# The stacked left rows in one transfer each, and a table of attention pieces with a row per FFN pair

## The chip, the cores and the metric

The program runs on one core of one Trainium2 chip. The metric is the device time of one execution in microseconds (us); lower is better. Before the change it is 1098.47 us, the median of three runs (1098.16 to 1099.85).

Engines are named as in the profile: PE is the matrix engine (PEld its weight loads), DVE the vector engine, ACT the scalar engine, POOL the GpSimd engine, SP the engine that does nothing here but issue transfers. SP, ACT and POOL each issue DMA transfers into a queue of their own; the page calls SP's queue q1, ACT's q10 and POOL's q0.

## What is computed

One transformer block in float32 with its two branches in parallel, over 2048 tokens of 576 features:

```python
xn = _layernorm(x, axis=-1)
return x + _A_ref(xn, A_wqkv, A_wo) + _B_ref(xn, B_w1, B_b1, B_w2, B_b2)

# _A_ref: 32 heads of 18 features, each query sees 8 keys, two tokens apart
idx = pos[:, None] - off[None, :]            # off = arange(8) * 2
logits = jnp.where(mask[None, None, :, :], einsum("bhsd,bhswd->bhsw", q, kg) * scale, -1e9)
o = jnp.einsum("bhsw,bhswd->bhsd", softmax(logits), vg)      # then @ wo

# _B_ref: feed-forward (FFN) of 4608 hidden features, squared relu
h = jnp.einsum("bsd,df->bsf", x, w1) + b1
r = jnp.where(h > 0, h, 0)
out = jnp.einsum("bsf,fd->bsd", r * r, w2) + b2
```

## The kernel before

**Tiling.** The tokens are cut into four blocks of 512. Every float32 operand of a matmul is held as a high and a low part, and a product is made of three matmuls (high x high, high x low, low x high). The 576 features are 512 main ones, in four groups of 128, and 64 left over, the *left rows*.

**The FFN in pairs.** The 36 tiles of 128 hidden features are worked in 18 pairs (`ffn_pair`, L673), in two passes: pass 0 handles token blocks 0 and 1, pass 1 blocks 2 and 3. A pair makes its first-layer products by a scheme with seven block products in place of eight; the seven are called B11, T1, T2, T3, B21, B22 and T4, and come in this order (B22 and T4 change places in the first pair). Each is six matmuls of 128x512 (L698). Between them PE does the second layer of the pair before (L590), handed out by `work`. A pair takes about 17 us in pass 0.

**The left rows, stacked.** For pairs 0 to 2 (`PLAIN = 3`) the 64 left rows are added by matmuls of their own (L704). From pair 3 on, each of the seven products ends with one matmul more (L697, run at L698) whose 128 rows hold all four combinations of high and low parts of 32 left rows: `LW` is the weights' side, `ST` the tokens' side. The tokens' side is made once in a pass: `left_x` (L619) writes 64 rows of seven slots (one slot for each product, 512 numbers wide) to a DRAM scratch `stscr`, shown as `stk` in the profile, through POOL's queue. `load_stack` (L633) brings slots back to SBUF with every row twice: rows 0 to 63 into partitions 0 to 63, and the same rows into partitions 64 to 127. It is called in five places, from `part` (L706):

- pass 0, pair 1: slots 0 to 4 into a `kv` buffer (10,240 bytes a row), slot 5 into `xf` (2,048 bytes a row);
- pass 0, pair 2: slot 6 into `x4d` (2,048 bytes a row);
- pass 1, pair 1: slots 0 to 3 into a `w1r` buffer (8,192 bytes a row);
- pass 1, pair 2: slots 4 to 6 into the other `w1r` buffer (6,144 bytes a row).

`STACK` gives the slot of each product: T1 0, B11 1, B22 2, B21 3, T3 4, T2 5, T4 6. The first products that need the slots are those of pair 3 in each pass. The weights' side comes with `load_left_weights` (L655), tiles `mb`, `st` or `x`, read from a scratch shown as `lw`. Its source pattern also reads each row twice, but as `[NS * P, 2 * L], [0, 2], [1, n * P]`: 64 rows outermost, the repeat inside.

**What else the queues carry.** SP's queue carries, in program order, the second layer's weights (`w2r<-in_w`, L551, three buffers), in pass 0 also the first layer's weights (`w1r<-in_w`) and the stores of their split form (`w<-w1s`, L533) and of hidden tiles (`h<-r`, L777; `op<-h`, L766 and L769 in pass 1). ACT's queue brings the split first-layer weights back in pass 1 (`w1s<-w`, L536). POOL's queue carries attention's loads and stores and, in pass 0, the stores of the left weights (`lw<-st`, L652).

**The order on the engines** is written by hand: each engine runs its instructions in the order in which the kernel's code names them.

**Attention's pieces.** Attention runs on DVE (with one exponential on ACT for each group) as a generator, `attention` (L394), that is cut into 18 to 20 steps; `side(k)` (L441) runs the next k of them at the place in the order where it stands. Three tables set k: `PIECES[p]` at the start of pair p of pass 0, `SPOTS[p][i]` at six spots of pair p in pass 1 (`spot`, L793), and `LAST[k]` after step k of the block products behind pass 1 (`phase_blocks`, L1504). The spots of a pair lie after B11 and T1 (0), after T2 (1), after T3 (2), after B21 (3), after B22 (4) and at the end (5); in the first pair only spot 5 is used.

Of the kernel before, what the change touches and what calls it, by code (L numbers as in the profile page):

```python
# [8 lines left out]
F32 = mybir.dt.float32  # L9
# [10 lines left out]
TB = 512  # L20
# [12 lines left out]
L = P // G  # L33
# [9 lines left out]
NS = 7  # L43
PLAIN = 3
ROWS = {(4 * b - 1 + k // 3, k % 3): (b, h) for b in (2, 3) for k, h in ((0, 0), (2, 2), (3, 1), (5, 2), (6, 2))}
PIECES = (0, 0, 0, 2, 3, 4, 0, 3, 2, 0, 2, 2, 1, 0, 2, 2, 4, 5)
SPOTS = ('000001',) + ('110022', '110023', '110023', '110023') * 4 + ('110021',)
QUADS = ('01111110111110', '10100010101011', '00110111111111', '10010000111111', '00000000000001', '00110010101010')
LAST = '0000000000000111001010111111'
SINGLES = '12121212121200000000'  # L50
PAIRED = tuple(range(1, 16, 2))
SINGLE = tuple(p for p in range(NP) if p not in PAIRED)
# [7 lines left out]
def block_kernel(ctx: ExitStack, tc: tile.TileContext, x, xt, wqkv, wo, w1, b1, w2, b2, w1l, w2q, w2l, out):  # L60
    nc = tc.nc
# [53 lines left out]
    stscr = [dram.tile([2 * L, NS, TB], F32, name=f"stk{s}") for s in range(2)]  # L115
# [325 lines left out]
    def side(k, exp=True):  # L441

        while k > 0:
            if current[0] is None:
                if not queue or queue[0][0] not in landed:
                    return k
                name, make = queue.pop(0)
                current[:] = [make(), None, name]
                steps_done[0] = 0
            if current[1] == "exp" and not exp:  # L450
                return k
            try:
                current[1] = next(current[0])
                steps_done[0] += 1
                k -= 1
            except StopIteration:
                current[0] = None
        return 0
# [3 lines left out]
    def some_side(t):  # L462
        owed[0] += t
        while True:
            exp = current[1] == "exp"
            cost = COST[steps_done[0]] if current[0] is not None else COST[0]
            if owed[0] < cost / 2 or side(1):
                break
            owed[0] -= cost
            if exp or current[1] == "exp":  # L470
                break
# [128 lines left out]
    def dims(t, off, *ap):  # L600
        a = t[tuple(slice(0, 1) for _ in t.shape)]
        return bass.AP(tensor=a.tensor, offset=a.offset + off, ap=[*ap])
# [29 lines left out]

    def load_stack(s, t, i):  # L633
        n = min(t.shape[1], NS - i)
        for h in range(2):
            nc.sync.dma_start(t[2 * h * L:2 * (h + 1) * L, :n].bitcast(F32), stscr[s][:, i:i + n])
        for k, place in STACK.items():
            if i <= place < i + n:
                ST[k] = t[:, place - i]
# [33 lines left out]
    def ffn_pair(s, p, work, first=False):  # L673
# [32 lines left out]
        def part(i):  # L706
# [15 lines left out]
            if i == 2 - p and p in (1, 2) and s:  # L722
                load_stack(1, sb.tile([P, 4, TB], F32R, name="w1r", bufs=2), 4 * p - 4)
            if i == 2 and p == PLAIN - 1 and not s:
                load_stack(0, mt.tile([P, 1, TB], F32R, name="x4d"), 6)
# [7 lines left out]
            if (p, i) == (1, 2):  # L733
                load_stack(0, sb.tile([P, 5, TB], F32R, name="kv", bufs=3), 0)
                load_stack(0, sb.tile([P, 1, TB], F32R, name="xf"), 5)
# [57 lines left out]
        def spot(i):  # L793
            if s and (not first or i == 5):
                some_side(int(SPOTS[p][i]))

        if not first and not s:
            side(PIECES[p], False)
        spot(0)
# [276 lines left out]
    def load_h(s, p):  # L1076
        t = hs[s, p] = mt.tile([P, 2, 2, TB], F32R, name="h", bufs=3)
        nc.sync.dma_start(t[:, 1].rearrange("p f t -> p (f t)").bitcast(F32), hscr[s][p])
# [6 lines left out]
    def h_lo(s, p):  # L1085
        if p < NP:
            t = hs[s, p]
            tt(t[:, 1], t[:, 1].bitcast(F32), t[:, 0].bitcast(F32), ALU.subtract)
# [415 lines left out]
    def phase_blocks():  # L1504
# [28 lines left out]
        for k in range(len(ORDER)):  # L1533
# [54 lines left out]
            if k == 25:  # L1588
                load_h(1, SINGLE[1])
                h_hi(1, SINGLE[0])  # L1590
                h_lo(1, SINGLE[0])
            side(int(LAST[k]))
        load_h(1, SINGLE[2])
# [498 lines left out]
```

## Time and profile before

| what | value |
|---|---|
| median of three runs | 1098.47 us |
| the profiled execution's own time | 1099.84 us |
| its span, first to last instruction | 1098.1 us |
| PE busy | 1083.5 us, 4871 matmuls |
| DVE busy | 930.9 us (85%) |
| ACT, POOL busy | 570.7 us (52%), 160.0 us (15%) |
| granted TensorE clock, mean | 0.998 |
| DMA engines, mean busy share | 0.81 at 285 GB/s |

The profiled execution took 1.74 us more than its span and 1.37 us more than the median. The chain of work that ended last is PE's for 90% of the span. A row of a view names the line of the code, the engine, the operation and the tiles, `out<-in`; a tile has no buffer number, so `w1r` may be raw weights or, later, the stacked rows. "DMA share" is the mean over the core's 16 DMA engines. In the view of waits a row reads: engine, tile and line that waited `<-` what ended the wait: us in total, times, longest.

### The profile page before, as it was taken

The page shows a single profiled execution, that of the slowest core. Times are in us where ns is not written, and L with a number is a line of the kernel's source. Part 1 is how long each engine was busy: PE and PEld are TensorE (multiplying, and loading weights), DVE is VectorE, ACT ScalarE, POOL GpSimd, SP SyncE. Part 2 cuts the span into 40 slices and gives each one's busy share as a digit, 9 for nine tenths or more (in the row PEclk, how much of TensorE's full clock was granted, in tenths as well). Part 3 has the DMA queues.
Part 4 walks back from the last instruction along what each step waited for, and adds up shares of the span by engine and source line. Part 5 has one row for each costly group of instructions (what it writes and reads, how often), then busy time and mean ns, then how long its engine had stood idle before and what let it go on. Part 6 is the DMA issues. An engine that isn't in the chain of part 4 may idle for free.

```text
span 1098.1 us, 13935 instructions
## 1 busy us (share of the span) xinstructions
PE 1083.5 (99%) x4871; PEld 908.9 (83%) x4871; DVE 930.9 (85%) x1245; ACT 570.7 (52%) x800; POOL 160.0 (15%) x294
## 2 busy tenths in 40 slices
PE   9999999999999999999999998999999999999998
PEld 7998888888888888888799986888778888887887
DVE  7976899999988979999899676879688888888986
ACT  5545655666656564555344344555455555543332
POOL 5011220212130100003110301021021040000110
PEclk9999999999999999999999999999999999999999
DMA  8758997897998697876865989998988988566573
GB/s 284 256 198 304 302 403 275 320 356 285 328 342 311 222 387 238 282 247 219 304 219 164 359 299 308 383 334 333 377 291 327 361 322 313 177 206 213 203 235 100
DMA packets 106887, 312.53 MB, mean 285 GB/s; under 512 B 12865, under 2 KB 39489, under 8 KB 95169
## 3 DMA queue, kind: packets, MB, share of 16 engines
q1 hardware_dynamic: 70048, 198.75, 51.5%
q0 software_dynamic: 15584, 71.96, 18.0%
q10 hardware_dynamic: 21184, 40.94, 11.1%
q8 instruction: 38, 0.62, 0.2%
q14 instruction: 33, 0.26, 0.1%
HBM read 216.62 MB, written 94.98 MB: 284 GB/s over the span
## 4 chain that ended last, share of the span: by engine, by line
PE 90%; DVE 5%; DMA 3%; issue 1%; ACT 1%; POOL 0%; ACTq 0%; DVEq 0%; POOLq 0%
PE p L590 35%; PE p L698 34%; PE p L1187 9%; PE p L1514 6%; PE p L1843 2%; DMA w1s<-w 2%; PE p L1191 2%; DVE pr L128 1%; PE p L1898 1%; PE p L704 1%; DMA w2r<-in_wo 1%; DVE h L128 1%; PE p L1753 1%; DVE w2s L128 0%; DVE r L128 0%
## 5 line engine op out<-in xcount | busy, mean ns | idle before, releaser
L590 PE MATMUL p<-h,w2s 128*128 128x512 f32 x1618 | 389.6, 390 | 0.0
L590 PEld LDWEIGHTS p<-h,w2s 128*128 128x128 f32 x1618 | 303.7, 188 | 64.3 <-ACT h L749 0.5
L698 PE MATMUL p<-X,w1s 128*128 128x512 f32 x864 | 219.6, 390 | 1.5 <-DVE r L128 1.5
L698 PEld LDWEIGHTS p<-X,w1s 128*128 128x128 f32 x864 | 162.2, 188 | 35.8 <-DVE r L128 1.9
L698 PE MATMUL p<-S,w1s 128*128 128x512 f32 x648 | 167.2, 394 | 0.5 <-ACT p L786 0.5
L698 PEld LDWEIGHTS p<-S,w1s 128*128 128x128 f32 x648 | 121.1, 189 | 29.3 <-ACT r L806 2.9
L562 ACT ACTIVATE w2s<-w2r 128x640 fp32r<-128x640 f32 x132 | 96.7, 734 | 87.2 <-PE p L590 54.1
L434 POOL DMA_DIRECT2D o<-q x128 | 69.4, 620 | 466.3 <-DVE q L128 465.8
L128 DVE TENSOR_TENSOR w2s<-w2r,w2s 128x576 fp32r<-128x576 f32 (+1 forms) x133 | 99.8, 751 | 18.0 <-ACT w2s L562 17.8
L745 ACT ACTIVATE r<-r,b1t 128x512 f32<-128x512 f32 x72 | 52.1, 724 | 116.1 <-DVE r L128 114.1
L128 DVE TENSOR_TENSOR h<-h 128x1024 fp32r<-128x1024 f32 (+1 forms) x74 | 72.5, 989 | 21.3 <-ACT h L762 13.7
L128 DVE TENSOR_TENSOR pr<-lg,kv 128x1152 f32<-128x1152 f32 x64 | 86.7, 1355 | 1.3
L128 DVE TENSOR_TENSOR pr<-q,kv 128x1152 f32<-128x1152 f32 x64 | 86.7, 1355 | 1.1
L405 DVE TENSOR_REDUCE lg<-pr 128x64 f32<-128x1152 f32 x64 | 86.4, 1350 | 1.0
L128 DVE TENSOR_TENSOR r<-p,r 128x512 f32<-128x512 f32 (+2 forms) x81 | 55.0, 681 | 36.2 <-ACT r L831 18.2
L128 DVE TENSOR_TENSOR pr<-pr 128x576 f32<-128x576 f32 (+1 forms) x128 | 77.5, 605 | 3.1
L753 ACT ACTIVATE r<-r 128x1024 f32<-128x1024 f32 x56 | 59.2, 1057 | 0.9
L806 ACT ACTIVATE r<-p 128x512 f32<-128x512 f32 x36 | 21.5, 598 | 57.2 <-PE p L698 57.1
L128 DVE TENSOR_TENSOR w1s<-w1r,w1s 128x1024 fp32r<-128x1024 f32 (+2 forms) x42 | 46.2, 1102 | 5.6 <-ACT w1s L523 5.0
L831 ACT ACTIVATE r<-p 128x512 f32<-128x512 f32 x36 | 21.5, 599 | 54.1 <-PE p L698 54.1
L745 ACT ACTIVATE r<-p,b1t 128x512 f32<-128x512 f32 x72 | 48.2, 671 | 0.0
L128 DVE TENSOR_TENSOR h<-r,h 128x1024 fp32r<-128x1024 f32 (+2 forms) x35 | 39.9, 1146 | 7.6 <-ACT r L753 6.0
(263 smaller groups left out, 1488.2 us busy)
## 6 DMA issues: line engine op xcount, KB each, us to landing
kv<-kvq POOLq DMA_DIRECT2D x32, 1296.0 KB, 9.6
w2r<-in_w SPq DMA_DIRECT2D x112, 320.0 KB, 4.1
w<-w1s SPq DMA_DIRECT2D x21, 1024.0 KB, 7.1
w1s<-w ACTq DMA_DIRECT2D x19, 1024.0 KB, 8.0
h<-r SPq DMA_DIRECT2D x28, 512.0 KB, 6.5
h<-h SPq DMA_DIRECT2D x28, 512.0 KB, 4.0
w<-w1s SPq DMA_DIRECT2D x15, 768.0 KB, 9.4
w1s<-w ACTq DMA_DIRECT2D x15, 768.0 KB, 7.7
```

What stands on the lines that cost most here:

```text
L128: return nc.vector.tensor_tensor(out=out, in0=a, in1=b, op=op)
L405: nc.vector.tensor_reduce(out=lg[:, j * HG:(j + 1) * HG].rearrange("p a w -> p w a"), in_=pr.rearrange("p w (a d) -> p w a d", d=DH), axis ...
L434: nc.gpsimd.dma_start(rows[:, i], q[i * L:(i + 1) * L, :, a:z])
L562: nc.scalar.activation(w2s[stream[i]][:, :DE], raw2[i], AF.Copy)
L590: nc.tensor.matmul(yp[b][c], v, a, start=c not in yb[b], stop=c in last and c not in [o[0] for o in ops[i + 1:]], skip_group_check=True)
L698: nc.tensor.matmul(to, l, r, start=start and i == 0, stop=i == len(mm) - 1, skip_group_check=True)
L745: nc.scalar.activation(to, a, AF.Relu, bias=b1t[:, f:f + 1])
L753: nc.scalar.activation(r, r, AF.Square)
L1187: nc.tensor.matmul(to, l[:, js], r, start=start and n == 0, stop=n == len(mm) - 1, skip_group_check=True)
L1191: nc.tensor.matmul(to, v[:, js], ws[LEFT, f][:, n], start=False, stop=n == 1, skip_group_check=True)
L1514: nc.tensor.matmul(p, l, r, start=id(p) not in begun, stop=stop, skip_group_check=True)
L1843: nc.tensor.matmul(p[:, :QW], l, r, start=k == 0, stop=k == len(mm) - 1)
```

## The change

There are two edits. The first makes one transfer of the two halves in `load_stack`: the source pattern reads the 64 rows, then the same 64 rows again (a step of 0, twice, outermost), into all 128 partitions of the tile. The same bytes move; the five calls issue five transfers in place of ten. The second edit changes the three tables that place attention's pieces: one number of `PIECES` (pair 14), one place of `LAST`, and `SPOTS`, which becomes a row for each of the 18 pairs. Pass 1 gets 115 steps where it had 114, the block products one fewer.

```diff
-PIECES = (0, 0, 0, 2, 3, 4, 0, 3, 2, 0, 2, 2, 1, 0, 2, 2, 4, 5)
-SPOTS = ('000001',) + ('110022', '110023', '110023', '110023') * 4 + ('110021',)
+PIECES = (0, 0, 0, 2, 3, 4, 0, 3, 2, 0, 2, 2, 1, 0, 3, 2, 4, 5)
+SPOTS = ('000002', '110022', '110023', '010023', '110023', '110022', ...
...
-        for h in range(2):
-            nc.sync.dma_start(t[2 * h * L:2 * (h + 1) * L, :n].bitcast(F32), stscr[s][:, i:i + n])
+        nc.sync.dma_start(t[:, :n].rearrange("p s c -> p (s c)").bitcast(F32),
+                          dims(stscr[s], i * TB, [0, 2], [NS * TB, 2 * L], [1, n * TB]))
```

`dims` builds an access pattern by hand, a list of (step, count) from the outermost to the innermost; `L` is 32.

The first place is SP's queue in pass 0, around pair 1 and 2. `kv`, `xf` and `x4d` are the stacked rows, `mb` and `x` the left weights of pairs 3 and 4, `w` and `h` stores to DRAM. Before:

```order
L643 DMA st<-in_w1l 128x512
L636 DMA kv<-stk_150 64x2560 x2
L636 DMA xf<-stk_150 64x512 x2
L663 DMA mb<-lw_152 128x1x896
L777 DMA h_162<-r_1274 128x1024
L551 DMA w2r<-in_w 128x640
L533 DMA w_116<-w1s 128x2048
L551 DMA w2r<-in_w 128x640
L506 DMA w1r<-in_w 128x1024
L533 DMA w_117<-w1s 128x1536
L636 DMA x4d<-stk_150 64x512 x2
```

And now:

```order
L643 DMA st<-in_w1l 128x512
L635 DMA kv<-stk_150 128x1x2560
L635 DMA xf<-stk_150 128x1x512
L663 DMA mb<-lw_152 128x1x896
L777 DMA h_162<-r_1274 128x1024
L551 DMA w2r<-in_w 128x640
L533 DMA w_116<-w1s 128x2048
L551 DMA w2r<-in_w 128x640
L506 DMA w1r<-in_w 128x1024
L533 DMA w_117<-w1s 128x1536
L635 DMA x4d<-stk_150 128x1x512
```

Nothing has changed places; each pair of 64-row transfers is one of 128 rows.

The second place is SP's queue in pass 1, pairs 1 and 2, where both `w1r` are the stacked rows and `st` is the left weights of pair 3. Before:

```order
L551 DMA w2r<-in_w 128x640
L636 DMA w1r<-stk_151 64x2048 x2
L663 DMA st<-lw_152 128x1x896
L636 DMA w1r<-stk_151 64x1536 x2
L766 DMA op_157<-h 128x2048
```

And now:

```order
L551 DMA w2r<-in_w 128x640
L635 DMA w1r<-stk_151 128x1x2048
L663 DMA st<-lw_152 128x1x896
L635 DMA w1r<-stk_151 128x1x1536
L766 DMA op_157<-h 128x2048
```

Here too the order is the same, with four transfers become two.

The third place is DVE in pass 1, from the sum behind B22 of pair 9 (the first `r<-p,r`) to the sum behind T3 of pair 10 (the second one), which frees the bank that B22 of pair 10 writes: `sm` and `lg` are attention's softmax, `pr` its products, `h<-h` the low parts of hidden tiles, `w2s` that of the second layer's weights. Before:

```order
L128 TENSOR_TENSOR r_6717<-p_6659,r_6698 128x512
L128 TENSOR_TENSOR h<-h 128x512 x2
L416 TENSOR_REDUCE sm<-lg 128x32
L417 RECIPROCAL sm<-sm 128x32
L128 TENSOR_TENSOR lg<-lg,sm 128x256
L128 TENSOR_TENSOR pr<-lg,kv 128x1152
L128 TENSOR_TENSOR q<-pr 128x144
L128 TENSOR_TENSOR h<-h 128x512 x2
L128 TENSOR_TENSOR pr<-lg,kv 128x1152
L128 TENSOR_TENSOR w2s<-w2r,w2s 128x576
L128 TENSOR_TENSOR r_6831<-p_6763,r_6807 128x512
```

And now:

```order
L128 TENSOR_TENSOR r_6714<-p_6654,r_6693 128x512
L416 TENSOR_REDUCE sm<-lg 128x32
L417 RECIPROCAL sm<-sm 128x32
L128 TENSOR_TENSOR lg<-lg,sm 128x256
L128 TENSOR_TENSOR pr<-lg,kv 128x1152
L128 TENSOR_TENSOR q<-pr 128x144
L128 TENSOR_TENSOR h<-h 128x512 x2
L128 TENSOR_TENSOR pr<-lg,kv 128x1152
L128 TENSOR_TENSOR h<-h 128x512 x2
L128 TENSOR_TENSOR w2s<-w2r,w2s 128x576
L128 TENSOR_TENSOR r_6829<-p_6766,r_6804 128x512
```

The first two `h<-h` stood ahead of the softmax and one product step; now they stand behind them. (The additions `pr<-pr` between a `pr<-lg,kv` and its `q<-pr` are left out in both.)

More of the change, by code (lines that the diff above doesn't have):

```diff
@@ L45 @@
 ROWS = {(4 * b - 1 + k // 3, k % 3): (b, h) for b in (2, 3) for k, h in ((0, 0), (2, 2), (3, 1), (5, 2), (6, 2))}
-PIECES = (0, 0, 0, 2, 3, 4, 0, 3, 2, 0, 2, 2, 1, 0, 2, 2, 4, 5)
-SPOTS = ('000001',) + ('110022', '110023', '110023', '110023') * 4 + ('110021',)
+PIECES = (0, 0, 0, 2, 3, 4, 0, 3, 2, 0, 2, 2, 1, 0, 3, 2, 4, 5)
+SPOTS = ('000002', '110022', '110023', '010023', '110023', '110022', '110023', '100024', '010024', '120022', '110023', '110023', '110023', '110022', '110023', '110023', '110123', '010021')
 QUADS = ('01111110111110', '10100010101011', '00110111111111', '10010000111111', '00000000000001', '00110010101010')
-LAST = '0000000000000111001010111111'
+LAST = '0000000000000111001010011111'
 SINGLES = '12121212121200000000'
```

## Prediction

> **What bounds the kernel now.** I read the page's first part, then the view of PE's waits (who waited `<-` for what: us in total, times, longest).
>
> ```profile
> span 1098.1 us, 13935 instructions
> PE 1083.5 (99%) x4871; PEld 908.9 (83%) x4871; DVE 930.9 (85%) x1245; ACT 570.7 (52%) x800; POOL 160.0 (15%) x294
> PE p L704 <- DMA w1s<-w: 4.0, 1, 4.0
> PE p L1187 <- DVE h L1063: 2.0, 1, 2.0
> PE p L698 <- DVE r L128: 1.5, 1, 1.5
> PE p L698 <- ACT p L786: 0.5, 1, 0.5
> ```
>
> PE works through 99% of the span, so the matmuls bound the kernel and no edit here takes one away. PE's waits are few and single: the longest, 4.0 us, is for a transfer, and 1.5 + 0.5 us of the others lie in pass 1. So a gain is a few us at most, while a loss has no such limit: any transfer that lands late stops PE one for one.
>
> The timeline of PE and that of the queues show the long wait in its place, pass 1, beside the stacked rows.
>
> ```profile
> 651.82 0.33 SPq L551 DMA_DIRECT2D w2r<-in_w  x1
> 652.37 1.40 SPq L636 DMA_DIRECT2D w1r<-stk  x2
> 655.71 0.33 ACTq L536 DMA_DIRECT2D w1s<-w  x1
> 656.54 0.55 SPq L663 DMA_DIRECT2D st<-lw  x1
> 657.19 1.20 SPq L636 DMA_DIRECT2D w1r<-stk  x2
> 662.49 0.33 ACTq L536 DMA_DIRECT2D w1s<-w  x1
> 669.71 0.72 PE L704 MATMUL p<-x,w1s 128*128 128x512 f32 x2 [4.03 <-DMA w1s<-w]
> 674.36 0.33 ACTq L536 DMA_DIRECT2D w1s<-w  x1
> 686.22 0.39 PE L698 MATMUL p<-w1r,st 128*128 128x512 f32 x1
> 667.00:680.00 13.00, 10.29 (x38) 8.33 (x39) 6.82 (x12) 1.90 (x3) 1.13 (x3) 0.87 1.01 319
> ```
>
> The weights issued at 655.71 land 14 us later, behind a full set of DMA engines, and PE waits 4.03 us for them. The last row (from the table by windows; the columns behind the busy times are granted clock, DMA share and GB/s) shows what such a wait costs beyond itself: the clock was 0.87 over 13.0 us, 13.0 x 0.13 = 1.7 us more.
>
> The cause lies in the halves. In pass 0 the same load stands nearly alone, and the DMA view of 130 to 150 us gives busy share and GB/s in 40 slices of 0.5 us:
>
> ```profile
> 127.28 0.33 SPq L643 DMA_DIRECT2D st<-in_w1l  x1
> 127.72 1.14 SPq L636 DMA_DIRECT2D kv<-stk  x2
> 128.91 1.31 SPq L636 DMA_DIRECT2D xf<-stk  x2
> 130.33 0.57 SPq L663 DMA_DIRECT2D mb<-lw  x1
> DMA  8996999996799999999999999979999999999999
> GB/s 246 246 266 143 246 246 225 184 246 127 152 256 309 255 331 414 426 398 418 478 442 414 406 449 449 430 316 487 415 413 418 385 430 442 430 410 365 352 254 306
> 136.87 0.55 POOL L652 DMA_DIRECT2D lw<-st  x1 [17.25 <-ACT st L607]
> 142.52 0.39 PE L698 MATMUL p<-kv,mb 128*128 128x512 f32 x1
> 156.85 0.39 PE L698 MATMUL p<-x4d,mb 128*128 128x512 f32 x1
> 130.00:136.00 6.00, 6.00 (x28) 4.95 (x28) 5.80 (x11) 4.53 (x7) 0.00 (x0) 1.00 0.97 215
> ```
>
> While the 64-row halves move, the 16 engines are 0.97 busy and yet move 215 GB/s; from the 15th slice on they are as busy and move about 416 GB/s, 26 GB/s for one engine. Half of the partitions take half the rate, so a transfer to all 128 could run twice as fast, if all 16 engines carry it.
>
> **What decides: how many engines carry the new transfer.** [...] The new source pattern is 2 x 64 x a row, with the count of 2 outermost; the tile's is 128 x a row. What the DMA view tells of how transfers are dealt out, and of the packets of SP's queue and of all:
>
> ```profile
> DMA packets 179, 0.61 MB, mean 197 GB/s; under 512 B 16, under 2 KB 16, under 8 KB 144
> mb<-lw SPq DMA_DIRECT2D x1, 448.0 KB, 8.2
> q1 hardware_dynamic: 70048, 198.75, 51.5%
> DMA packets 106887, 312.53 MB, mean 285 GB/s; under 512 B 12865, under 2 KB 39489, under 8 KB 95169
> ```
>
> The first row is the DMA view of 186.0 to 189.1 us, in which one `w2r` of 128 rows ends: 16 small packets stand beside its rows, one for each engine, I take it. All large transfers of before have 32, 64 or 128 as their outermost count on both sides, `mb<-lw` too, which repeats each row inside of 64. So no row prices a count of 2; the ends are 16 engines and 2. The nearest row by bytes is `mb<-lw`, but it differs in exactly the outermost count. I take 2, since the cut that the pattern itself offers first gives two shares of 64 rows, and dealing the inner 64 out would need another rule for this case than for the rest. This is a choice, and its chance below says so.
>
> [...]
>
> **The change part by part, with two engines.** Each engine then carries half of the bytes at 26 GB/s. All transfers of SP's queue wait behind their share on those two engines, as in before each landed behind its forerunner.
>
> Two rows of the DMA view, for the times from issue to landing (KB each, median us), are used below:
>
> ```profile
> w2r<-in_w SPq DMA_DIRECT2D x1, 320.0 KB, 9.1
> st<-in_w1l SPq DMA_DIRECT2D x1, 256.0 KB, 2.7
> ```
>
> *Pass 0.* The stack is issued at 127.72; `st<-in_w1l` alone landed after 2.7 us of which 262,144 bytes at 416 GB/s are 0.6, so about 2 us pass before data move: 129.7. Slots 0 to 4 are 128 x 10,240 bytes, 655,360 for each engine: 25.2 us. Slot 5: 131,072, 5.0 us. `mb<-lw`, 458,752 bytes over 16, 28,672: 1.1 us, and two `lw<-st` of the same size between them 2.2 us (the second is issued 3 us behind the first). Together 33.5: landing at 163.2. The first matmul that needs both starts at 142.52: PE waits **20.7 us**, and the clock costs **1.7** more. Next is `x4d`: behind it stand `h`, three weight loads, two stores and its own 5.0 us, 13.6 in all, 176.8; it is needed at 156.85 + 20.7 = 177.6, so nothing is added, with 0.8 us to spare. The other transfers behind (`w2r`, `w`) are needed a pair (17 us) later and move along with PE.
>
> *Pass 1.* The queue ahead is full until the `w2r` of 651.82 lands, 9.1 us later: 660.9. Then slots 0 to 3, 524,288 bytes an engine, 20.2 us; `st` 1.1; slots 4 to 6, 393,216, 15.1; and from ACT's queue, which shares the engines, two loads of 65,536 and one of 49,152, 5.0 + 1.9. Together 43.3: 704.2. T2 of pair 3 needs slot 5 at 686.22: **18.0 us**, again with **1.7** of clock. The old wait at 669.71 stays inside this sum: that load has its own queue and lands sooner, but what PE gains there it waits out at T2.
>
> *The five issues saved* are 0.5 to 0.7 us each on SP, which is not the late one: 0.
>
> *Moved pieces.* The 1.5 us wait is B22 of pair 10 waiting for DVE's sum behind T3. DVE's timeline there:
>
> ```profile
> 785.35 1.42 DVE L128 TENSOR_TENSOR h<-h 128x512 f32<-128x512 f32 x2 [4.80 <-ACT h L762]
> 794.01 0.68 DVE L128 TENSOR_TENSOR r<-p,r 128x512 f32<-128x512 f32 x1
> ```
>
> DVE stood idle 4.80 us for `h<-h`, with the softmax queued behind it. The new order puts softmax and product ahead of `h<-h`, into that idle time, and only one more group of additions (1.55 us) ahead of the sum. The wait should go: **-1.5**, bounds -2.0 (the 0.5 us wait goes too) and +4 (each product step is 1.36 us, and one or two of the other moved steps may land ahead of a sum that PE needs).
>
> Sum: 20.7 + 1.7 + 18.0 + 1.7 - 1.5 = 40.6 us. Made against the profiled execution, 1099.84 + 40.6 = 1140.4; that execution is 1.37 above the median, so **1139.1 us**.
>
> Bounds. The highest slices but two, 449 GB/s, give 28 for one engine: waits of 18.3 and 14.9, no loss of clock, -2.0: 1129.7. The mean rate of SP's queue, 198.75 MB in 51.5% of 16 x 1098.1 us, is 22.0: waits of 26.9 and 25.9, 3.4 of clock, 0 for the pieces: 1154.7. The likeliest case by itself: 1129 to 1155.
>
> **The rivals.**
>
> *Sixteen engines, faster.* Speaks for it: rate and share above. The place is the 4.03 us wait at 669.71. Slots 0 to 3 are 1.05 MB, 4.9 us at 215 and 2.5 at 416; the second load's part ahead of the weights saves some 0.7. The weights land 3.1 us sooner, the wait shrinks to about 1, and the clock loss goes (the 2.0 us wait in the first fence left the clock at 1.00): 3.1 + 1.7 + 1.5 = 6.3, **1092.2 us**, 1091 to 1097. Against it: the count of 2. It decides from about eight engines: slots 0 to 5 are then 7.6 us, `mb` lands at 140.6, before 142.52.
>
> *Sixteen engines, no change.* The bytes stay, DMA is 1.01 busy there with or without, and the wait may only move to the next load. **1098 us**, 1096.5 to 1100.5.
>
> *The pieces cost.* The transfers are harmless, but a product step of 1.36 us stands ahead of a sum in some of the 16 pairs: three such, **1102.5 us**.
>
> **How the numbers follow.** Two engines 0.67, sixteen and faster 0.21, no change 0.08, the pieces 0.04. A measurement of this kernel can tell 0.2%, 2.2 us, from no change. So faster 0.21, same 0.08, slower 0.71. The range must reach over both signs: 1091 to 1155 leaves out the ends of the first two cases, about 1 in 10 or a little more.
>
> **What would show each step.** With two engines the page's small packets ("under 512 B") fall by 10 x 16 - 5 x 2 = 150 to 12,715; with sixteen by 80, to 12,785. PE's waits should name `kv<-stk` or `mb<-lw` with some 20 us, and `w1r<-stk` with some 18, and the wait for `w1s<-w` and that for DVE's `r` be gone; the stacked loads should land 25 to 45 us after issue. It is wrong if they land within 8 us, or if they land late and PE does not wait.

## The result, and the profile after

The changed kernel takes 1157.63 us, the median of 4 runs (1155.99 to 1159.1), beside 1099.16 us (4 runs) for the kernel before: a ratio of 1.0524, with an interval of 1.0493 to 1.0555. The forecast was 1139.1 us, 1091 to 1155: right in its direction and in the two engines, but too low; the result lies above its range. The profiled execution took 1157.96 us, its span 1156.3.

The page of the changed kernel; the first number behind a queue's kind is its packets:

```profile
span 1156.3 us, 13924 instructions
PE 1087.2 (94%) x4871; PEld 912.7 (79%) x4871; DVE 931.9 (81%) x1245; ACT 571.0 (49%) x800; POOL 160.0 (14%) x294
DMA packets 106736, 312.53 MB, mean 270 GB/s; under 512 B 12714, under 2 KB 39338, under 8 KB 95018
q1 hardware_dynamic: 69898, 198.75, 48.8%
```

SP's queue went from 70,048 packets to 69,898, which is 150 fewer: ten transfers with a small packet for each of 16 engines became five with one for each of two. So two engines carry each of the new transfers. The records of landings in the trace say the same: that of `kv<-stk` comes in two parts, at 161.97 and 162.18 us, where those of other transfers come in sixteen. PE is busy 3.7 us longer than the 1083.5 of before, and 94% of the span in place of 99%; the rest is waits. PE's waits, all that the view lists:

```profile
PE p L698 <- DMA mb<-lw: 28.7, 1, 28.7
PE p L698 <- DMA st<-lw: 19.3, 1, 19.3
PE p L698 <- DMA w1r<-stk: 14.8, 1, 14.8
PE p L1670 <- DVE lg L1663: 2.1, 1, 2.1
```

Three waits for transfers stand where there was one of 4.0 us; that one, the 2.0 us for `h` and the 1.5 and 0.5 us are gone. These four make 64.9 us. With the 2.1 us wait, which was there before too, and two of 0.7 and 0.2, the old ones made 11.0. So 53.9 us of the 58.2 that the span grew are waits and 3.7 are PE's longer busy time.

Where they lie is shown by the timelines of the changed kernel, SP's issues (start, us that the issue took) and PE's first matmuls behind each wait:

```profile
128.57 0.64 SPq L635 DMA_DIRECT2D kv<-stk  x1
129.27 0.53 SPq L635 DMA_DIRECT2D xf<-stk  x1
129.90 24.06 SPq L663 DMA_DIRECT2D mb<-lw  x1
154.06 5.10 SPq L777 DMA_DIRECT2D h<-r  x1
...
682.70 0.56 SPq L635 DMA_DIRECT2D w1r<-stk  x1
683.45 2.37 SPq L663 DMA_DIRECT2D st<-lw  x1
685.92 1.91 SPq L635 DMA_DIRECT2D w1r<-stk  x1
694.38 26.27 SPq L766 DMA_DIRECT2D op<-h  x1
```

```profile
172.07 0.80 PE L698 MATMUL p<-kv,mb 128*128 128x512 f32 x1 [28.68 <-DMA mb<-lw]
725.05 0.76 PE L698 MATMUL p<-w1r,st 128*128 128x512 f32 x1 [19.32 <-DMA st<-lw]
745.24 0.79 PE L698 MATMUL p<-w1r,st 128*128 128x512 f32 x1 [14.83 <-DMA w1r<-stk]
```

Pair 3 of pass 0 starts its first stacked product at 172.07 in place of 142.52. The transfers that PE waits for first in each pass are ordinary ones, `mb<-lw` and `st<-lw`: they land in sixteen parts, but two of the sixteen come behind the stacked rows. Of `st<-lw`, fourteen parts were there by 691.77 us and the last two at 723.35 and 724.92; the two parts of the stacked load ahead of it landed at 722.23 and 723.50. The issues of 24.06 and 26.27 us were not foreseen: SP itself stood still while the stacked rows ahead of them in its queue were being worked off (0.58 us for `mb<-lw` in the kernel below that has the load in ACT's queue).

The table by windows (the last three columns are granted clock, DMA share, GB/s) and the DMA view of 128 to 175 us (KB each, median us from issue to landing):

```profile
130.00:136.00 6.00, 6.00 (x29) 4.95 (x28) 5.11 (x10) 4.46 (x7) 0.00 (x0) 1.00 0.16 61
150.00:154.00 4.00, 0.00 (x0) 0.00 (x0) 0.00 (x0) 0.00 (x0) 2.76 (x6) 0.50 0.35 99
160.00:172.00 12.00, 0.00 (x0) 0.00 (x0) 0.00 (x0) 0.00 (x0) 0.00 (x0) 0.50 0.98 323
```

```profile
kv<-kvq POOLq DMA_DIRECT2D x1, 1296.0 KB, 12.7
lw<-st POOLq DMA_DIRECT2D x2, 448.0 KB, 7.1
mb<-lw SPq DMA_DIRECT2D x1, 448.0 KB, 42.1
o<-q POOLq DMA_DIRECT2D x4, 48.0 KB, 5.2
o<-q POOLq DMA_DIRECT2D x4, 24.0 KB, 8.4
```

In the window of 130 to 136 us, where the halves had the engines busy at 0.97 for 215 GB/s, it is now 0.16 and 61 GB/s, about two engines' worth. `mb<-lw` lands 42.1 us after its issue; fourteen of its sixteen parts were there by 162.65 us, the last two at 171.69 and 172.02. And POOL's attention transfers, `kv<-kvq` and eight `o<-q`, run in the same stretch: their packets take turns with the stacked rows on the two engines (those of `kv<-kvq` end there at 164.97 us, on the fourteen others before 160.1), and the forecast's sum did not hold them.

### The profile page after: what moved, and what is told of

It reads as the page before. It is cut to its first block, busy times and chain, and to the rows that moved or that the text cites. A ratio compares the mean times of both kernels' runs of the same rounds, so it can differ in the third digit from the quotient of the medians.

```text
span 1156.3 us, 13924 instructions
## 1 busy us (share of the span) xinstructions
PE 1087.2 (94%) x4871; PEld 912.7 (79%) x4871; DVE 931.9 (81%) x1245; ACT 571.0 (49%) x800; POOL 160.0 (14%) x294
## 2 busy tenths in 40 slices
DMA packets 106736, 312.53 MB, mean 270 GB/s; under 512 B 12714, under 2 KB 39338, under 8 KB 95018
## 3 DMA queue, kind: packets, MB, share of 16 engines
q1 hardware_dynamic: 69898, 198.75, 48.8%
## 4 chain that ended last, share of the span: by engine, by line
PE 88%; DMA 9%; another core or an unknown queue 1%; DVE 1%; issue 0%; POOL 0%; ACT 0%; POOLq 0%; SPq 0%; ACTq 0%
PE p L590 34%; PE p L698 30%; PE p L1187 9%; PE p L1514 8%; DMA mb<-lw 4%; DMA st<-lw 4%; PE p L1843 2%; DMA w1s<-w 2%; PE p L1191 2%; PE p L1753 1%; PE p L1898 1%; PE p L704 0%; PE p L1670 0%; DVE lg L405 0%; DVE pr L128 0%
## 5 line engine op out<-in xcount | busy, mean ns | idle before, releaser
L698 PE MATMUL p<-X,w1s 128*128 128x512 f32 x864 | 219.7, 390 | 0.2
L698 PEld LDWEIGHTS p<-X,w1s 128*128 128x128 f32 x864 | 162.1, 188 | 34.7 <-ACT r L745 0.5
L698 PE MATMUL p<-S,w1s 128*128 128x512 f32 x648 | 169.0, 397 | 0.0
L698 PEld LDWEIGHTS p<-S,w1s 128*128 128x128 f32 x648 | 122.7, 192 | 28.8 <-ACT r L806 2.7
L128 DVE TENSOR_TENSOR h<-h 128x1024 fp32r<-128x1024 f32 (+1 forms) x74 | 72.6, 990 | 19.0 <-ACT h L762 10.7
L806 ACT ACTIVATE r<-p 128x512 f32<-128x512 f32 x36 | 21.5, 598 | 75.3 <-PE p L698 75.1
L786 ACT ACTIVATE p<-p 128x512 f32<-128x512 f32 x36 | 20.9, 582 | 64.8 <-PE p L698 62.3
L374 POOL DMA_DIRECT2D kv<-kvq x32 | 18.6, 587 | 205.5 <-DVE pr L128 161.4
```

The costliest lines, as they stand in the source:

```text
L128: return nc.vector.tensor_tensor(out=out, in0=a, in1=b, op=op)
L698: nc.tensor.matmul(to, l, r, start=start and i == 0, stop=i == len(mm) - 1, skip_group_check=True)
```

## The experiments

The theory is that the outermost count of the source sets how many engines carry a transfer, that all that is queued on these few comes late, and that PE waits for that. Lines from L630 on are moved by up to four in some of these kernels (L702 is then L698). The kernel before was run beside each: medians of 1098.5 to 1099.2 us, 1100.2 in the last.

### Each edit alone

The first edit with the old tables (`e_load`), and the second with the two halves (`e_pieces`); the diffs are the two parts of the diff above.

> The one-transfer load alone, with the old tables. Theory: all of the loss stays, 1156 to 1161 us, with PE waiting some 29 us before pair 3 of pass 0 and some 34 us in pass 1; page q1 has 69,898 packets. Rival (part of the loss is the pieces'): 1120 to 1150 us.

> The new tables of attention's pieces alone, with the stacked rows in two 64-row transfers as before. Theory (two DMA engines carry the new transfers, and that is the whole loss): the tables cost nothing and remove the wait of 1.5 us for DVE's sum in pair 10, so 1095 to 1098 us. Rival (the moved pieces bring part of the loss): 1101 us or more.

The new load alone: 1162.15 us (ratio 1.0573, 1.0554 to 1.0593), 62.9 us slower. The new tables alone: 1094.99 us (0.9964, 0.995 to 0.9978), 4.2 us faster. So the whole loss is the load's, and the tables are a gain. The first of the two lies 1.2 us above the range that was expected, the second at the lower edge of its range. Of PE's waits in the kernel with the new tables alone these are left:

```profile
PE p L698 <- DMA mb<-lw: 2.4, 1, 2.4
PE p L1670 <- DVE lg L1663: 2.1, 1, 2.1
PE p L1187 <- DVE h L1063: 0.6, 1, 0.6
PE p L698 <- DMA w1s<-w: 0.4, 2, 0.2
```

The waits for DVE's `r` and ACT's `p` are gone, as forecast; that for `w1s` shrank from 4.0 to 0.4, with 2.4 us for `mb<-lw` in its place, which was not.

### One pass at a time

The new load for pass 0 only, and for pass 1 only (`s == 1`), halves in the other, old tables:

```diff
+        if s == 0:
+            nc.sync.dma_start(t[:, :n].rearrange("p s c -> p (s c)").bitcast(F32),
+                              dims(stscr[s], i * TB, [0, 2], [NS * TB, 2 * L], [1, n * TB]))
+        else:
             for h in range(2):
```

> The change's load (count of 2 outermost) in pass 0 alone; pass 1 loads in halves, old tables. Theory (two engines, and the loss is the wait of PE in each pass with its clock, so that the passes add): 28.7 us of wait and 1.7 of clock, as in the changed kernel's pass 0: 1129 to 1131 us, SP's packets 70,048 - 6 x 16 + 3 x 2 = 69,958. Rival (what pass 0 delays comes back in pass 1, or the other way round): 1120 us or less, or 1140 and more.

> The change's load in pass 1 alone; pass 0 loads in halves, old tables. Theory: two waits of some 17 and 15 us with 1.7 us of clock, less the 4.0 us wait and its 1.7 of clock that go: 1126 to 1132 us, SP's packets 70,048 - 4 x 16 + 2 x 2 = 69,988; together with the load in pass 0 alone the losses make the 63 us of the new load with the old tables. Rival (the two passes do not add): outside 1120 to 1136 us.

Pass 0 alone: 1130.82 us (ratio 1.0286, 1.0259 to 1.0313), 32.1 us. Pass 1 alone: 1132.87 us (1.0304, 1.0279 to 1.0328), 34.1 us; the second is 0.9 us above what was expected. The packets are 69,958 and 69,988, as expected. The sum, 66.2 us, is 3.3 above what the load does in both; each interval is about 3 us to either side, so the passes add as far as this can tell. PE's waits of pass 1 alone:

```profile
PE p L702 <- DMA st<-lw: 17.8, 1, 17.8
PE p L702 <- DMA w1r<-stk: 15.1, 1, 15.1
...
716.58 0.79 PE L702 MATMUL p<-w1r,st 128*128 128x512 f32 x1 [15.05 <-DMA w1r<-stk]
```

The last row is T2 of pair 3, from PE's timeline. Here pass 0 is undisturbed, so it compares directly with the 686.22 of before: 30.4 us later.

### The repeat inside, on sixteen engines

```diff
-                          dims(stscr[s], i * TB, [0, 2], [NS * TB, 2 * L], [1, n * TB]))
+                          dims(stscr[s], i * TB, [NS * TB, 2 * L], [0, 2], [1, n * TB]))
```

The same bytes and still a zero step, but 64 is now the outermost count. Each row goes to two neighbouring partitions, so other rows meet in the products. With the old tables, and with the new:

> One transfer of 128 rows with the same bytes and the same step of zero, but with the 64 rows outermost and the repeat inside, so that row r goes to partitions 2r and 2r+1 (the stacked products then pair other rows than they should; all work stays). Old tables. Theory (the outermost count decides how many engines carry it): 16 engines, q1 has 70048 - 80 = 69,968 packets, the load of slots 0 to 4 lands within 6 us in pass 0, and the wait of 4.0 us in pass 1 shrinks: 1092 to 1097 us. Rival (reading the same rows twice in one transfer is slow by itself, whatever the count): some 1150 us or more.

> One transfer of 128 rows with the repeat inside 64 rows (so other rows meet in the products), and the new tables: the whole change as it would be on sixteen engines. Theory (load and tables both mend the same 4.0 us wait in pass 1, and each alone gains 4.2 us): 1091 to 1094 us, not the sum of the two gains. Rival (they add): 1088 to 1091 us.

1094.82 us with the old tables (ratio 0.9962, 0.9948 to 0.9976) and 1089.62 us with the new (0.9914, 0.9886 to 0.9942). SP's packets are 69,968 in both, 80 fewer than before: sixteen engines. With the old tables `kv<-stk` lands 8.2 us after its issue, later than the 6 that were expected, but not the 33.6 of the changed kernel. So here the count that stands outermost decided, not that a step is zero. The expectation that the two gains overlap was a miss: 4.2 and 4.4 us alone, 9.1 together, and with both PE has no wait for a transfer left:

```profile
PE p L1670 <- DVE lg L1663: 2.1, 1, 2.1
PE p L1187 <- DVE h L1063: 0.9, 1, 0.9
```

### The same load from ACT's queue

Slots 0 to 5 of pass 0 by the change's pattern, issued by `nc.scalar` in place of `nc.sync`; all else in halves, old tables.

> Two engines carry slots 0 to 5 in pass 0 (the load of the change), but it is issued on ACT's queue; slot 6 and pass 1 load in halves, old tables. Theory (the two engines' total of work counts, whichever queue brings it): PE still waits 20 to 30 us at pair 3, now for kv<-stk or xf<-stk, SP's issue of mb<-lw is no longer held for 24 us and it lands early: 1118 to 1132 us. Rival (what hurts is that SP's queue stands still behind the load): mb<-lw lands early and PE waits at most 15 us: 1115 us or less.

1128.49 us (ratio 1.027, 1.0239 to 1.03), as the theory has it. SP is not held now and `mb<-lw` lands 15.2 us after its issue, but:

```profile
138.42 1.27 DVE L128 TENSOR_TENSOR st<-st 128x128 f32<-128x128 f32 x4 [11.75 <-DMA st<-in_w1l]
...
142.82 2.93 PE L702 MATMUL p<-X,w1s 128*128 128x512 f32 x6 [6.19 <-DVE r L128]
166.77 0.76 PE L702 MATMUL p<-kv,mb 128*128 128x512 f32 x1 [14.36 <-DMA kv<-stk]
177.51 0.50 PE L702 MATMUL p<-xf,mb 128*128 128x512 f32 x1 [3.00 <-DMA xf<-stk]
```

The first row is of DVE's timeline, the others of PE's. PE waits for the stacked rows themselves, and before that for DVE, which stood 11.75 us behind `st<-in_w1l`: a load of SP's that landed 10.7 us after its issue, where it took 2.5 in the changed kernel. 6.2 + 14.4 + 3.0 = 23.6 us of waits where the changed kernel has 28.7: by this comparison, that the load shares SP's queue is a minor part, the two engines' work the larger.

### Four and eight engines

```diff
-        for h in range(2):
-            nc.sync.dma_start(t[2 * h * L:2 * (h + 1) * L, :n].bitcast(F32), stscr[s][:, i:i + n])
+        nc.sync.dma_start(t[:, :n].rearrange("p s c -> p (s c)").bitcast(F32),
+                          dims(stscr[s], i * TB, [0, 4], [NS * TB, 32], [1, n * TB]))
```

For eight it is `[0, 8], [NS * TB, 16]`; in the third kernel `[10 * NS * TB, 4]` stands for `[0, 4]`. With the zero steps part of the combinations is left out of the products, with the step of 10 rows other rows meet; the work stays the same.

> The stacked load is again one transfer of 128 rows with a zero step outermost, but of a count of 4: 32 scratch rows are read four times, so the right half of the combinations is missing from the products; old tables. Theory (the outermost count is the number of engines): four engines carry it, each a quarter of the bytes. Pass 0: 129.7 + 12.6 + 2.5 + 3.3 = 148.1 us against the need at 142.5, so PE waits about 5.5 us for mb<-lw, and at most 1.7 us of clock go with it; pass 1 about even, since slots 0 to 3 take 10.1 us in place of 20.2 and the old wait of 4 us goes or stays: 1101 to 1109 us. SP's packets: 70,048 - 160 + 5 x 4 = 69,908. Rival (any zero step outermost costs what a count of 2 costs, through something else than the number of engines): 1140 us or more.

> The same with a count of 8: 16 scratch rows are read eight times, so most of the combinations are missing from the products; old tables. Theory: eight engines, 6.3 + 1.3 + 3.3 us behind 129.7 is 140.6, ahead of the need at 142.5: no wait in pass 0, and the old wait of 4 us in pass 1 shrinks as with sixteen: 1094 to 1099 us, SP's packets 70,048 - 160 + 40 = 69,928. Rival (a zero step outermost as such): 1140 us or more.

> As the load with a count of 4 outermost, but the outer step is 10 scratch rows in place of 0: the four engines read rows b, b + 10, b + 20 and b + 30 at the same time and never the same row at once (so other rows meet in the products); old tables. It tells apart why four engines took 0.71 us for a packet of 10,240 bytes where two took 0.39. Theory A (several engines that read the same row at the same time hold one another up): 0.39 us a packet, mb<-lw lands near 148 us, PE waits about 5.5 us in pass 0: 1101 to 1110 us. Theory B (it is the four engines' writes, or the rows as such): 0.7 us a packet as before, 1132 to 1140 us. Theory C (only a zero step confines a load to few engines): SP's packets above 69,908 and no wait.

SP's packets are 69,908, 69,928 and 69,908: four, eight and four engines, with a step that isn't zero too. But the first two times were misses: 1136.23 us (ratio 1.034, 1.0318 to 1.0363) and 1115.84 us (1.0166, 1.014 to 1.0192) are some 30 and 20 us above the theory's. The third, 1135.56 us (1.0334, 1.0301 to 1.0368), is in the range of its theory B. The trace's packets of 10,240 bytes in pass 0 tell how: 0.39 us in the median with two engines (26.6 GB/s), 0.71 with four, 0.77 with eight, 0.60 with four and the step of 10 rows (0.71 until 142 us, as with the zero step). It isn't that they read the same row at once, then, since with the step of 10 rows they don't. What was left: how they lie on the partitions.

### Which partitions are written at the same time

Four transfers of 32 rows, each to every fourth partition, all 16 engines and the new tables; the left weights' rows are stored in another order, so that every product is made of the same rows as in the kernel before:

```diff
-        for h in range(2):
-            nc.sync.dma_start(t[2 * h * L:2 * (h + 1) * L, :n].bitcast(F32), stscr[s][:, i:i + n])
+        for q in range(4):
+            nc.sync.dma_start(t[q::4, :n].bitcast(F32), stscr[s][q % 2::2, i:i + n])
...
-            dims(lwscr[i], k * L * NS * P, [NS * P, L], [2 * L * NS * P, G], [1, NS * P]), part.rearrange("p s c -> p (s c)")))
+            dims(lwscr[i], k * NS * P, [2 * NS * P, L], [2 * L * NS * P, G], [1, NS * P]), part.rearrange("p s c -> p (s c)")))
```

> New tables; the stacked rows come in four transfers of 32 rows for each place, each to every fourth partition, and the left weights' rows are stored in another order so that the products meet as in the kernel before. SP issues 20 transfers in place of 10 (each some 0.6 us), SP's packets 70,048 - 160 + 320 = 70,208. Theory A (a transfer is slow when it fills only one half of the partitions): a packet of 10,240 bytes takes 0.39 us in place of 0.78, and it comes out as the one transfer with the repeat inside, less the longer issue: 1088 to 1093 us. Theory B (short transfers, or the scratch's rows as such, are slow): 0.7 us and more a packet, and the time is that of the new tables alone or above: 1094 to 1100 us.

1089.74 us (5 runs, 1088.42 to 1090.1; ratio 0.9914, 0.9898 to 0.9929): it beats both kernels, and comes out as the load with the repeat inside. A packet takes 0.39 us in the median, beside 0.78 in the halves. The page and the table by windows of this kernel:

```profile
span 1088.4 us, 13948 instructions
PE 1081.3 (99%) x4871; PEld 908.0 (83%) x4871; DVE 931.9 (86%) x1245; ACT 571.0 (52%) x800; POOL 159.8 (15%) x294
q1 hardware_dynamic: 70208, 198.75, 51.0%
```

```profile
130.00:136.00 6.00, 6.00 (x29) 4.95 (x28) 5.42 (x9) 4.86 (x7) 0.00 (x0) 1.00 0.89 284
```

The other side of it: two engines, as in the change, but writing partitions 32 apart in place of 64 apart (other rows meet in the products; old tables):

```diff
         for h in range(2):
-            nc.sync.dma_start(t[2 * h * L:2 * (h + 1) * L, :n].bitcast(F32), stscr[s][:, i:i + n])
+            nc.sync.dma_start(t[2 * h * L:2 * (h + 1) * L, :n].rearrange("p s c -> p (s c)").bitcast(F32),
+                              dims(stscr[s], i * TB, [NS * TB, 2], [2 * NS * TB, L], [1, n * TB]))
```

> Two transfers of 64 rows as in the kernel before, but with a count of 2 outermost (the even scratch rows go to the first 32 partitions of a half, the odd ones to the second 32, so other rows meet in the products); old tables. Two engines carry everything, as in the changed kernel, but at each moment they write partitions 32 apart in place of 64 apart. SP's packets 70,048 - 160 + 20 = 69,908. Theory A (partitions p and p + 32 of one half share a way in, which halves the rate of two engines that write them together): 0.7 to 0.8 us a packet of 10,240 bytes at first, in place of 0.39, and unless the two fall out of step soon, a time well above that of the new load with the old tables: 1175 to 1225 us. Theory B (two engines have the full rate wherever they write): 0.39 us a packet and 1157 to 1167 us.

One run: 1168.8 us, between the two expectations. Its packets took 0.74 us in the median up to 143 us (39 of the 128) and 0.39 from then on, where the first packets of POOL's `lw<-st` come between them. The table by windows shows the slow part:

```profile
130.00:136.00 6.00, 6.00 (x29) 4.95 (x28) 5.54 (x10) 4.71 (x8) 0.00 (x0) 1.00 0.12 29
136.00:142.00 6.00, 6.00 (x28) 4.99 (x27) 5.79 (x10) 3.65 (x6) 1.10 (x2) 1.00 0.38 131
```

29 GB/s where the changed kernel, with two engines as well, moves 61. So, if each of the two engines carried one of the two shares, two that wrote partitions 32 apart held one another up, and two that wrote 64 apart did not. If the shares were dealt out in the order of the rows, the other slow loads had engines that wrote 32 apart too: four engines with 32 rows each (0.71 us a packet), eight with 16 (0.77) and, in the halves, sixteen with 4 (0.78). The change's two, 64 apart, took 0.39.

Two things do not fit so simply, so this reading is argued and not shown. The trace does not say which engine writes which partition. If sixteen engines took the 128 partitions of the load with the repeat inside in eights, in order, engines four apart would write 32 apart too, yet its packets took 0.42 us with the old tables and 0.39 with the new; by the same count so would those of the four transfers over all partitions, with 0.39. So the account needs them to be dealt out otherwise there, which no run tested. And in the last kernel the slow part ends although both engines still start their packets together (at 144.29 and 144.31 us, 0.385 us each). By a count of the packets, one of the two is then one row ahead, so that they would write 31 or 33 partitions apart; whether that ends the slow part is open.

### The scratch written twice

The store writes 128 rows, each row twice, by a second store on SP's queue, and the load is a plain one of 128 rows; new tables. In both passes, and in pass 1 only (pass 0 in halves):

```diff
-                nc.gpsimd.dma_start(dims(stscr[s], k * NS * TB + i * TB, [2 * NS * TB, L], [1, TB]), part[:, i])
+                for c, queue in enumerate((nc.gpsimd, nc.sync)):
+                    queue.dma_start(dims(stscr[s], (2 * c * L + k) * NS * TB + i * TB, [2 * NS * TB, L], [1, TB]), part[:, i])
```

> The scratch holds the 64 rows twice (14 more stores of 64 KB in each pass, on SP's queue), and each load is one transfer of 128 plain rows. New tables. Theory: 16 engines; the wait for the first-layer weights in pass 1 shrinks and that of pair 10 goes, 1090 to 1097 us, unless the 14 stores delay the loads behind them by more than the 3 us gained, then 1097 to 1103. Rival (a transfer of 128 rows is slower than two of 64): 1105 us or more.

> New tables; in pass 1 alone the scratch is written with 128 rows, each row twice, by 7 more stores of each part on SP's queue, and read by plain transfers of 128 rows; pass 0 loads in halves. Theory (a plain 128-row load goes at the full rate, and the stores of pass 1's stack have time): the 2.4 us that the new tables alone leave at pair 2 of pass 1 go, and the rest stays: 1091 to 1094 us. Rival (the 14 more stores hold SP's queue or the DMA engines, and something else is late for them): 1095 us or more.

In both passes: 1098.55 us (ratio 1.0001, 0.9989 to 1.0013): the tables' gain of 4.2 us is gone. In the profiled execution, the slowest of the twelve at 1103.16 us, PE waits 4.8 us for DVE's `r` in pass 0, where no such wait was; that the added stores do this was only argued. In pass 1 alone: 1093.98 us (0.9955, 0.9938 to 0.9971); the 2.4 us wait for `mb<-lw` is gone, but 2.1 us for `h` (L1187, L1191 there) and 1.5 for `w2s` stand there, so it is no more than 1 us from the tables alone, which the intervals do not tell apart.

## Why the prediction was right, and where it failed

**Right: two engines, and what they do.** The count of 2 gives two engines (69,898 packets in SP's queue; 12,714 small packets, where 12,715 were forecast), each at 26 GB/s (0.39 us for 10,240 bytes). The waits named, for `mb<-lw` and `w1r<-stk`, are there, the old ones for `w1s` and DVE's `r` are not, `x4d` adds none, and the stacked loads landed late: `kv<-stk` 33.6 us after its issue, the first of pass 1 40.8 us (682.70 to 723.50), where 25 to 45 were forecast. The second of pass 1 took 59 us (685.92 to 745.20). No row of before had a count of 2, so the forecast's two engines were a choice; the packets bear it out.

**Right in its sum only: the clock.** 1.7 us for each pass were forecast, 3.4 together; PE's busy time grew by 3.7. But it grew by 4.2 in the kernel with the load in pass 0 alone and by 2.0 with that in pass 1 alone, so the two terms are not borne out one by one, and that the sum fits is in part luck.

**Failed: the lists of work on the two engines.** "Together 33.5: landing at 163.2" for pass 0 and "Together 43.3: 704.2" for pass 1 are the steps that were too small. `mb<-lw` landed at 129.90 + 42.1 = 172.0, 8.8 us later than forecast, and T2 of pass 1 (by the kernel with the load in pass 1 alone) ran at 716.58, 12.4 us later.

*Pass 0.* The packets of the changed kernel's trace give the list that the two engines worked through. A record does not name its engine, but the stacked rows are all theirs, and of each other transfer two sixteenths, most of which run when the fourteen others have ended (for `lw<-st` a sixteenth of the whole is taken). For one engine, in us:

| transfer | forecast | trace |
|---|---|---|
| slots 0 to 4 | 25.2 | 27.8 |
| slot 5 | 5.0 | 5.6 |
| two `lw<-st` | 2.2 | 2.3 |
| `mb<-lw` | 1.1 | 1.6 |
| `kv<-kvq` | not counted | 3.5 |
| eight `o<-q` | not counted | 0.9 |
| sum | 33.5 | 41.7 |

The first packet starts at 130.2 in place of 129.7 and the last one ends at 171.7, so these packets fill the whole time: the two engines were never short of work, and SP's standing still did not delay `mb<-lw` there. Of the 8.2 us more, 4.4 are POOL's attention transfers, which the forecast left out: it counted SP's transfers and, of POOL, the stores that stood in the row it quoted. Another 2.6 are the stacked rows themselves. The 15 of their packets that start between 155.25 and 160.25 us, while the fourteen other engines carry `kv<-kvq`, take 0.58 to 0.82 us in place of 0.39. Why they slow each other was not tried.

*Pass 1* is known less well. There the first stacked packet starts at 657.7, 3.2 us earlier than the 660.9 of the forecast, so the list was 15.6 us too short. By bytes at 26 GB/s, POOL's `kv<-kvq`, `o<-q` and `q<-kvq` are 4.6 of them. A fourth load of ACT's, `w1s<-w` at 697.24 (65,536 bytes an engine), is 2.5: PE's waiting itself lets further transfers come into the time that is being summed. The packets of slots 0 to 3 took 0.37 us in the mean where 26 GB/s is 0.315, some 3.6 us for the 64 of one engine. The other 5 us are not divided further. And `st<-lw`, which stands behind the first stacked load and is needed before T2, was waited for first, 17.8 of the 32.9 us; it does not add to what T2 waits for, but the forecast had only `w1r<-stk` there.

**Failed: the size of the pieces.** -1.5 us was forecast, with -2.0 as the bound; the tables gained 4.2 us (2.4 to 5.5) alone, and 4.5 beside the new load (1162.15 against 1157.63). The wait looked at went as described; that the 4.0 us wait for `w1s` shrinks as well was not seen, and how the tables do that was not tried.

**The sum.** In waits, 20.7 + 18.0 - 1.5 = 37.2 us were forecast and 53.9 measured; that is nearly all of the 17.6 us between 40.6 and 58.2. The upper bound, 1154.7, took a lower rate (22.0) for the same short list, so it missed for the same reason. It also took 0 for the pieces, where +4 had been named as their bound; with +4 it would have been 1158.7 and held the result, but by luck, since the pieces gained.

**The rivals.** Sixteen engines would have been 1092.2 us by the forecast; with the repeat inside it is 1089.62, and by transfers over all partitions 1089.74. "It decides from about eight engines" was wrong: with eight it is 1115.84, slower than before, since a packet took 0.77 us there and not 0.39. The reading that halves of the partitions take half the rate was right in its number (0.78 us); that engines wrote partitions 32 apart is a likely reason, argued above and not shown.

## What to carry to other kernels

Before transfers are merged, look at the outermost count of the source: with 2, 4 and 8 that many engines carried the transfer, with 32, 64 and 128 sixteen did. The repeat of two outside took 1157.63 us, inside of the 64 rows 1089.62, so here it belonged inside of the large count. Two things set a transfer's rate here, how many engines carried it and how their rows lay on the partitions: 61 GB/s with the change's two engines, 215 in the halves and 284 in the four transfers over all partitions, all from 130 to 136 us. With the new tables, those four short transfers beat the two that fill one half each, 1089.74 against 1094.99 us. And when a resource becomes scarce, its list of users is every queue's, of the whole stretch that the delay lasts, not only what stands in the rows around the edit: of the 8.2 us that the list of pass 0 lacked, 4.4 were POOL's.

## What the hardware showed that was not expected

- With the stacked rows of two engines in SP's queue, issues behind them on that queue took long themselves: 24.06 us for `mb<-lw` and 26.27 for `op<-h`, where the issues of the kernel before that are shown above took 0.3 to 0.7 for each transfer. What came behind was issued only then, `h<-r` at 154.06 us (130.99 before) and `w2r<-in_w` at 721.21. With the same load in ACT's queue, SP's issue of `mb<-lw` took 0.58 us.
- One packet of 10,240 bytes took 0.39 us with the change's two engines, 0.78 in the halves, and 0.71 and 0.77 with four and eight engines; the busy share showed nothing of it (0.97 for 215 GB/s in the halves, 0.89 for 284 in the four transfers over all partitions).
- The granted clock was 0.50 while PE stood for long (150 to 154 and 160 to 172 us), and still PE's busy time grew by no more than 3.7 us over all three waits. With the load on ACT's queue it grew by 7.7 (1091.2 against 1083.5); why was not tried.
